# Row-layout loads, a spectrum with the frequency innermost, and two-frequency products in a long-convolution kernel

## The chip, the cores and the metric

The kernel runs on one core of a Trainium2 chip. The metric is the device time of one execution in microseconds. Before the change it was 288.6 us, the median of 3 runs (286.54 to 289.76). Every ratio compares a kernel with the kernel before on the same chip in the same rounds. Experiments of different rounds are compared by these ratios.

## The reference, cut to what matters

```python
# q = k = v: [1, 2048, 512] bf16; shift_k: [512, 4]; ssm_k: [512, 2048]; ssm_D: [512]
k_shift = sum(k_pad[:, t:t+S, :] * shift_k[:, ks-1-t] for t in range(4))   # causal conv of 4 taps
kv   = k_shift * v
kv_f = rfft(pad(kv, 2S));  kf_f = rfft(pad(ssm_k, 2S)).T
y    = irfft(kv_f * kf_f)[:, :S] + kv * ssm_D
h    = x + layernorm(x) * y                     # x = q
out  = h + relu(layernorm(h) @ w1) @ w2
```

The kernel makes each transform in two stages of matrix products. A token is 64 a + b (a and n1 run over 32, b and n2 over 64), and a channel is 128 rg + 64 d + g (four row groups rg, two halves d, 64 g). A "frequency" below is one k1 of the 32 of the first stage.

## The kernel before

"# ..." marks a cut.

```python
# start: tokens in rows of 512 channels, 16 tokens a partition; conv in 8 pieces of 2x512
for c in range(NT // RC):
    acc = pr.tile([P, RC, D], BF16, name="acc")
    # ... 4 multiplies with wbc, 3 adds, all on nc.vector ...
    nc.vector.tensor_tensor(out=vt[:, rr, :], in0=acc[:], in1=vt[:, rr, :], op=ALU.mult)
# ssm_k: 64 TensorE transposes, evicted by ACT into kfl[P, g, d, b]
for q in range(8):
    pst = psum.tile([P, 8, P], BF16, tag="ps", name="pst")
    # ... 8 transposes ...
    nc.scalar.copy(out=kfl[:, :, :, 8*q:8*q+8], in_=pst[:].rearrange("p i (dp g) -> p g dp i", dp=2))
# product k*v: 64 TensorE shuffles into PSUM, then ACT writes the stage's layout
xfl = xflp.tile([P, 64, 2, 64], BF16, name="xfl")        # [g, d, token]
    # ... matmul with ident as lhsT ...
    nc.scalar.copy(out=xfl[:, :, :, n0:n0+4], in_=pcs[a][:].rearrange("p i (dp g) -> p g dp i", dp=2))

kf = slotB.tile([P, DC, 32, 64, 2], F32R, tag="B", name="kf")   # re/im innermost, frequency outside
def store_kf(k1, ps):                                            # D is added here, on DVE
    nc.vector.tensor_tensor(out=kf[:, :, k1, :, 0], in0=ps[:, 0, :]..., in1=dtab_b[:], op=ALU.add)
    nc.scalar.copy(out=kf[:, :, k1, :, 1], in_=ps[:, 1, :]...)

def product(k1, ps):                                             # one frequency at a time
    t12 = prod.tile([P, 2, DC * 64], F32R, name="t12")
    nc.vector.tensor_tensor(out=t12v[:, :, 0:NV, :], in0=u[:, :, 0:NV, :], in1=k_same[:, :, 0:NV, :], op=ALU.mult)
    # ... t34 with re/im swapped; the last quarter of both on nc.gpsimd ...

for t in range(NT):                                              # 16 statistics ahead of the inverse
    nc.vector.bn_stats(out=st1[:, t, :], in_=xh[:, t, :])
    # ...
for g in range(64):                                              # first inverse stage
    nc.tensor.matmul(out=pso, lhsT=kf[:, :, :, g, 0], rhs=dre[:], start=True, stop=False)
    nc.tensor.matmul(out=pso, lhsT=kf[:, :, :, g, 1], rhs=dim[:], start=False, stop=True)
    # ... 3 of 4 evictions on ACT, 1 on DVE ...
```

## Time and profile before

| stage | from (us) | to (us) | limit |
|---|---|---|---|
| set-up, loads, conv | 0 | 42.5 | phases, sines, evictions one behind the other |
| first and second stage of k | 42.5 | 82 | ACT, then TensorE |
| first stage of x | 81.9 | 94.8 | TensorE |
| products with second stage of x | 96.5 | 131.2 | TensorE, DVE near it |
| first inverse stage | 131.9 | 168 | evictions, statistics |
| second inverse stage, MLP | 168 | 287.4 | TensorE |

The time of a stage is read from the first and last matmul of its tile. In profile lines PE is TensorE, PEld its weight loads, DVE VectorE, ACT ScalarE, POOL GpSimd, and L253 is line 253 of the kernel. These are groups of instructions of the kernel before: line, engine, operation, output from inputs, shapes, count, then busy us and mean ns of one, then idle time ahead of them.

```profile
L334 DVE TENSOR_TENSOR t<-ps,kf 128x384 fp32r<-128x384 f32 x32 | 17.6, 550 | 1.9 <-ACT usb L333 1.7
L263 DVE TENSOR_TENSOR vt<-acc,vt 128x1024 bf16<-128x1024 bf16 x8 | 5.4, 685 | 0.0
L283 ACT CAST xfl<-pc 128x512 bf16<-128x512 f32 x16 | 8.4, 1105 | 0.0
L99 PEld LDWEIGHTS <-xfl 32*128 32x128 bf16 x256 | 6.5, 106 | 0.1
```

A product of 384 f32 elements took 550 ns, and the product k*v, 1024 bf16 elements written in order, 685 ns: 0.67 ns an element. The layout of xfl was written by ACT, from PSUM, in runs of 4 tokens.

### The profile page before, as it was taken

How to read it: one execution, taken by the hardware profiler on the slowest of the kernel's cores; microseconds unless marked ns; L12 is line 12 of the kernel's file. 1: busy time of each engine (PE TensorE's matmuls, PEld its weight loads, DVE VectorE, ACT ScalarE, POOL GpSimd, SP SyncE). 2: the span in 40 equal slices, each digit the busy share in tenths (PEclk: the TensorE clock that was granted, in tenths of full speed). 3: DMA queues.
4: the chain of work that ended last, by engine and by line, in shares of the span. 5: the costliest groups of instructions: out<-in, count | busy, mean ns of one | idle time of the engine just before them, and what ended most of it. 6: DMA issues, size and time to landing. Idle time of an engine off the chain costs nothing.

```text
span 287.4 us, 7594 instructions
## 1 busy us (share of the span) xinstructions
PE 225.3 (78%) x3098; PEld 156.9 (55%) x3108; DVE 196.2 (68%) x449; ACT 152.9 (53%) x327; POOL 48.0 (17%) x97
## 2 busy tenths in 40 slices
PE   2027007889986699988999385999999998999994
PEld 0027005529975699977999273544544554444441
DVE  4899999985896599996836936578294258233221
ACT  1039999998885278877966313464352045113000
POOL 9921000000000389983000000000000000000000
PEclk9999555556995599996899757589999999999999
DMA  5699400000000000029156000000000200020122
GB/s 120 150 344 229 98 0 6 5 2 0 2 3 5 2 2 2 2 66 208 22 183 211 0 2 5 2 2 1 5 0 5 57 18 0 18 57 0 38 56 55
DMA packets 7876, 14.25 MB, mean 50 GB/s; under 512 B 2210, under 2 KB 5634, under 8 KB 7714
## 3 DMA queue, kind: packets, MB, share of 16 engines
q1 hardware_dynamic: 4898, 11.31, 15.5%
q10 hardware_dynamic: 2944, 2.46, 3.0%
q8 instruction: 24, 0.39, 0.6%
q14 instruction: 10, 0.08, 0.1%
HBM read 11.67 MB, written 2.10 MB: 48 GB/s over the span
## 4 chain that ended last, share of the span: by engine, by line
PE 60%; ACT 11%; DVE 9%; issue 3%; DMA 2%; ACTq 0%; DVEq 0%; SPq 0%
PE ps2m L465 12%; PE ps1m L454 12%; PE pz L422 7%; ACT a1k L270 5%; PE psi L391 4%; PE psi L392 4%; DVE st L382 3%; PE ps L112 3%; PE ps L114 3%; PE ps L115 3%; PE ps L113 3%; PE pt L444 1%; DMA xh<-in_A_q_dram 1%; ACT xfl L283 1%; DVE a1x L304 1%
## 5 line engine op out<-in xcount | busy, mean ns | idle before, releaser
L454 PE MATMUL ps1m<-hlnT,w 128*128 128x512 bf16 (+1 forms) x169 | 41.6, 387 | 2.1 <-ACT h1T L457 1.0
L465 PE MATMUL ps2m<-w,h1T 128*128 128x512 bf16 (+1 forms) x173 | 38.4, 379 | 0.2
L468 DVE TENSOR_TENSOR o<-ps2m,xh 128x512 bf16<-128x512 f32 x16 | 11.1, 692 | 29.6 <-PE ps2m L465 17.8
L391 PE MATMUL psi<-dre,kf 128*128 128x256 f32 x64 | 26.4, 412 | 5.3 <-DVE bp L396 3.1
L454 PEld LDWEIGHTS <-w 128*128 128x128 bf16 (+1 forms) x176 | 17.0, 102 | 23.2 <-issue 7.8
L457 ACT ACTIVATE h1T<-ps1m 128x512 bf16<-128x512 f32 (+1 forms) x24 | 14.4, 599 | 27.4 <-PE ps1m L454 24.7
L465 PEld LDWEIGHTS <-h1T 128*128 128x128 bf16 (+1 forms) x176 | 17.2, 98 | 20.8
L422 PE MATMUL pz<-bp,ecore 32*32 32x128 f32 x1024 | 25.2, 393 | 3.5 <-ACT zt L428 2.1
L336 POOL TENSOR_TENSOR t<-usb,kf 128x128 fp32r<-128x128 f32 x32 | 15.1, 473 | 73.3 <-ACT usb L333 71.6
L392 PE MATMUL psi<-dim,kf 128*128 128x256 f32 x64 | 25.4, 397 | 0.0
L99 PE MATMUL ps<-f_hi,kfl 32*128 32x64 bf16 x256 | 10.3, 234 | 18.5 <-ACT kfl L230 15.7
L391 PEld LDWEIGHTS psi<-dre,kf 128*128 128x128 f32 x64 | 20.0, 313 | 7.1 <-DVE bp L396 3.4
L394 ACT COPY bp<-psi 128x256 f32<-128x256 f32 x48 | 17.8, 372 | 9.3 <-PE psi L392 7.6
L428 ACT CAST zt<-pz 128x512 bf16<-128x512 f32 x16 | 8.2, 600 | 26.4 <-PE pz L422 26.4
L348 ACT CAST kf<-psy 128x512 fp32r<-128x512 f32 x32 | 20.1, 631 | 3.6 <-POOL t L336 1.4
L422 PEld LDWEIGHTS pz<-bp,ecore 32*32 32x32 f32 x1024 | 15.5, 117 | 10.4 <-issue 4.1
L392 PEld LDWEIGHTS psi<-dim,kf 128*128 128x128 f32 x64 | 20.3, 317 | 0.0
L433 DVE TENSOR_TENSOR gt<-zt,qln 128x512 bf16<-128x512 bf16 x16 | 6.5, 407 | 19.8 <-ACT zt L428 19.8
L334 DVE TENSOR_TENSOR t<-ps,kf 128x384 fp32r<-128x384 f32 x32 | 17.6, 550 | 1.9 <-ACT usb L333 1.7
L459 DVE TENSOR_SCALAR h1T<-ps1m 128x512 bf16<-128x512 f32 x20 | 13.6, 682 | 7.1 <-PE ps1m L454 7.1
L229 PE MATMUL pst<-ident,sk 128*128 128x128 bf16 x64 | 6.7, 299 | 14.0 <-DMA sk<-in_A_ssm_k_dram 14.0
L335 DVE TENSOR_TENSOR t<-ps,kf 128x384 fp32r<-128x384 f32 x32 | 17.5, 548 | 0.0
(133 smaller groups left out, 575.7 us busy)
## 6 DMA issues: line engine op xcount, KB each, us to landing
vt<-in_A_v_dram SPq DMA_DIRECT2D x16, 128.0 KB, 8.4
sk<-in_A_ssm_k_dram SPq DMA_DIRECT2D x1, 2048.0 KB
xh<-in_A_q_dram SPq DMA_DIRECT2D x4, 512.0 KB, 8.4
kh<-in_A_k_dram SPq DMA_DIRECT2D x13, 128.0 KB, 4.5
w<-in_B_w_dram SPq DMA_DIRECT2D x1, 1376.0 KB, 6.4
w<-in_B_w_dram ACTq DMA_DIRECT2D x1, 1280.0 KB, 9.6
out_dram<-o SPq DMA_DIRECT2D x32, 32.0 KB, 1.5
out_dram<-o ACTq DMA_DIRECT2D x32, 32.0 KB, 1.7
```

Of the source, the lines that this page charges most:

```text
L270: _stage1(nc, psum, kfl, f1hi, f1lo, a1k, lambda i, d, s: nc.scalar.copy(out=d, in_=s))
L334: nc.vector.tensor_tensor(out=t12v[:, :, 0:NV, :], in0=u[:, :, 0:NV, :], in1=k_same[:, :, 0:NV, :], op=ALU.mult)
L335: nc.vector.tensor_tensor(out=t34v[:, :, 0:NV, :], in0=u[:, :, 0:NV, :], in1=k_swap(0, NV), op=ALU.mult)
L336: nc.gpsimd.tensor_tensor(out=t12v[:, :, NV:DC, :], in0=usb[:], in1=k_same[:, :, NV:DC, :], op=ALU.mult)
L348: nc.scalar.copy(out=kf[:, :, k1, :, :].rearrange("p r g s -> p s r g"), in_=psy[:].rearrange("p s (r g) -> p s r g", r=DC))
L391: nc.tensor.matmul(out=pso, lhsT=kf[:, :, :, g, 0], rhs=dre[:], start=True, stop=False)
L392: nc.tensor.matmul(out=pso, lhsT=kf[:, :, :, g, 1], rhs=dim[:], start=False, stop=True)
L394: nc.scalar.copy(out=bp[:, g, :, :, :], in_=ps[:])
L422: nc.tensor.matmul(out=pz[32 * a:32 * a + 32, rg, l4, :], lhsT=ecore[rows, rho, n2, :], rhs=rhs, start=(rho == 0), stop=(rho == 1), tile_p ...
L454: nc.tensor.matmul(out=ps1[:fsz, :], lhsT=w1[:, c, fc * P:fc * P + fsz], rhs=hlnT[:, c, sc * SCW:(sc + 1) * SCW], start=(c == 0), stop=(c ...
L457: nc.scalar.activation(out=h1T[:fsz, fc, sc * SCW:(sc + 1) * SCW], in_=ps1[:fsz, :], func=ACT.Relu)
L465: nc.tensor.matmul(out=ps2[:], lhsT=h1T[:ksz, fc, t * P:(t + 1) * P], rhs=w2[:ksz, fc, :], start=(fc == 0), stop=(fc == NFC - 1))
```

## The change

The intent is to take work off the start and off the evictions. k, v and ssm_k are loaded straight into the layout of the first stage (a row group per 32 partitions), so 128 TensorE transposes and shuffles and 24 ACT evictions go away; DVE's product writes xfl itself. D is added by a small matmul in the first stage of k. The spectrum kf is stored as [re/im, g, rg, frequency], so that the first inverse stage loads its weights in order; two frequencies are handled per product. The order of instructions is set by hand. The diff, cut to its core:

```diff
-    kh = pp.tile([P, NT + 3, D], BF16, name="kh")            # 4 KB rows of tokens
+    pieces = [(0, 16), (16, 12), (28, 8), (36, 8), (44, 8), (52, 8), (60, 4)]
+            src = bass.AP(tensor=k_d.tensor, offset=k_d.offset + (n0 - h) * D + P * rg,
+                          ap=[[64 * D, 32], [D, rc + h], [1, P]])                # 256 B pieces
+            nc.sync.dma_start(out=kx[i][rows, 3 - h:rc + 3, :], in_=src)
 # ...
-        nc.scalar.copy(out=kfl[:, :, :, 8 * q:8 * q + 8], in_=pst[:].rearrange("p i (dp g) -> p g dp i", dp=2))
+                src = bass.AP(tensor=A_ssm_k.tensor, ..., ap=[[64, 32], [S, 32], [1, 64]])  # 128 B pieces
+                nc.sync.dma_start(out=kfl[32*rg:32*rg+32, 32*gh:32*gh+32, dp, :], in_=src)
 # ...
+    for pq in (lo, hi):
+        nc.gpsimd.tensor_single_scalar(out=cn[pq, :, pq], in_=cs[pq, :, pq].bitcast(F32), scalar=-1.0, op=ALU.mult)
 # ...
-            nc.scalar.copy(out=xfl[:, :, :, n0:n0 + 4], in_=pcs[a][:].rearrange("p i (dp g) -> p g dp i", dp=2))
+        eng = nc.gpsimd if i == 0 else nc.vector
+        eng.tensor_tensor(out=xfl[:, :, :, n0:n0 + rc].rearrange("p g d n -> p n d g"),
+                          in0=acc[:].rearrange("p n (d g) -> p n d g", d=2),
+                          in1=vx[i][:].rearrange("p n (d g) -> p n d g", d=2), op=ALU.mult)
 # ...
-    kf = slotB.tile([P, DC, 32, 64, 2], F32R, tag="B", name="kf")
+    kf = slotB.tile([P, 2, 64, DC, 32], F32R, tag="B", name="kf")
 # ...
+    def product(kp):
+        u = psum.tile([P, 2, 2, 256], F32, tag="u", name="u")
+        uj = u[:].rearrange("p s k j -> p s j k")
+            t = prod.tile([P, 2, 2, 256], F32R, tag="t%d" % swap, name="t")
+            tj = t[:].rearrange("p s k j -> p s j k")
+                eng.tensor_tensor(out=tj[:, :, j, :], in0=in0, in1=in1, op=ALU.mult)   # pairs of frequencies inside
 # ...
-    for t in range(NT):
-        nc.vector.bn_stats(out=st1[:, t, :], in_=xh[:, t, :])
+    for b in range(16):                       # first inverse stage, four g a block
+        # ... 8 matmuls with lhsT=kf[:, c, 4*b+i, :, :], one eviction of 1024 ...
+        if b >= 8:
+            ln1_stats(b - 8)
```

## The prediction

> **What bounds the kernel now.** I read the page, then the stage table (busy time per stretch), then the groups, waits and DMA packets of single stretches. Columns of the table: stretch, its length, busy us (instructions) of PE, PEld, DVE, ACT, POOL, granted TensorE clock, DMA share, GB/s.
>
> ```profile
> 0.00:16.00 16.00, 1.96 (x4) 0.43 (x4) 10.72 (x17) 1.28 (x1) 13.45 (x22) 1.00 0.61 164
> 16.00:27.00 11.00, 6.74 (x64) 6.60 (x64) 10.96 (x40) 7.54 (x15) 2.82 (x3) 1.00 1.05 276
> 27.00:42.50 15.50, 0.00 (x0) 0.00 (x0) 15.50 (x30) 15.38 (x22) 0.00 (x0) 0.56 0.32 71
> 42.50:59.50 17.00, 13.86 (x535) 9.10 (x536) 16.96 (x30) 15.76 (x34) 0.00 (x0) 0.50 0.02 4
> ...
> 64.00:82.00 18.00, 18.00 (x156) 17.80 (x144) 13.17 (x31) 14.86 (x38) 0.00 (x0) 0.84 0.00 1
> 82.00:96.50 14.50, 8.74 (x513) 6.85 (x512) 10.36 (x17) 8.94 (x18) 0.00 (x0) 0.66 0.02 4
> 96.50:126.50 30.00, 30.00 (x240) 30.00 (x241) 28.49 (x61) 23.55 (x58) 25.99 (x59) 0.93 0.01 2
> ...
> 131.90:154.00 22.10, 22.07 (x97) 21.78 (x98) 10.75 (x26) 17.43 (x44) 1.19 (x2) 0.86 0.57 161
> 154.00:168.00 14.00, 9.00 (x33) 7.42 (x32) 12.55 (x39) 6.10 (x15) 0.00 (x0) 0.78 0.09 28
> ```
>
> The rows are: set-up up to 42.5 us; first stage of k (ACT-bound: 32 evictions at 0.49 us); second stage of k from 64 (PE full); first stage of x; the products (PE full, DVE 28.5 of 30); the first inverse stage, 131.9 to 168. After 168 come second inverse and MLP, 119 us, which the change leaves alone. So no one engine bounds the whole; each stage has its own limit. The waits name three that need not be there:
>
> ```profile
> ACT f_f L67 <- DVE f_aph L60: 15.9, 1, 15.9
> PE ps L99 <- ACT kfl L230: 15.7, 1, 15.7
> DVE bp L396 <- PE psi L392: 12.3, 12, 2.2
> ```
>
> ACT stands idle to 17.9 us because the phase arithmetic is behind convolution work on DVE; then PE waits for the kfl evictions mixed among sines. The chain of waits shows the third loss: from 154.45 to 165.03 it runs through 16 bn_stats (0.66 us apart) with the last evictions of the inverse behind them. And the groups show a slow weight load:
>
> ```profile
> L391 PEld LDWEIGHTS psi<-dre,kf 128*128 128x128 f32 x64 | 20.0, 313 | 7.1 <-DVE bp L396 3.4 <-ACT bp L394 2.7 <-ACT kf L348 1.0
> L112 PEld LDWEIGHTS ps<-a1k,c2c 128*128 128x128 f32 x32 | 7.0, 218 | 0.5 <-issue 0.5
> ```
>
> Strided weights (kf with re/im innermost) take 313 ns, contiguous ones of the same size 218.
>
> [...] Trace: 2752-byte packets of w1 ran at 398 GB/s (110 ns each per engine, 16 engines), 1 KB packets of w2 at 348 (47 ns). A line through both gives 9 ns + 0.037 ns/B, so about 14 ns at 128 B and 18 ns at 256 B. But the only 128-byte packets of this trace, those of dtab_b, ran far below it, with the engines mostly idle (windows 2 to 3 us, then 152 to 154 us):
>
> ```profile
> DMA packets 287, 0.03 MB, mean 35 GB/s; under 512 B 287, under 2 KB 287, under 8 KB 287
> q1 hardware_dynamic: 287, 0.03, 21.4%
> DMA packets 672, 0.70 MB, mean 348 GB/s; under 512 B 0, under 2 KB 671, under 8 KB 671
> q10 hardware_dynamic: 671, 0.69, 108.2%
> ```
>
> That is some 350 packets/us (45 GB/s) once started. All of them read the same 1 KB of HBM, so I cannot tell a limit on packets from a hot spot. This is the main uncertainty. [...] loads to 32 partitions ran at 213 to 233 GB/s with engines full, those to 128 at 348 to 398. Every new k, v and ssm_k load has 32 partitions. [...] Trace: 240 matmuls of 256 columns in 30 us, 125 ns at clock 0.93[...] Trace: 128 elements 0.47 us, started 0.425 apart[...].
>
> **The change part by part.**
> *Start.* Removed: 64 transposes (6.7 us PE), 8 kfl evictions (7.6 us ACT), 64 shuffles of v with 16 evictions (8.4 us ACT), broadcast of the weights over PE, one of 5 DVE operations per pair of phase tables, the third sine table (8 x 0.63 us). Order is by hand: phases and sines first, convolution after. ACT has only 4 sines of 64x2048 (about 2 us each) and is free by some 20 us. Added: packets. ssm_k is read in 16,384 pieces of 128 B, k and v in 19,060 of 256 B (before: mostly 4 KB). By the fitted line: 16,384 x 14/16 + 19,060 x 18/16 ns = 14 + 22 = 36 us[...]. The second half of kfl is behind 24,308 packets: about 28 us. Then half of the first stage of k (8 evictions of 1024 elements at 0.92 = 7.4 us), and 18 us of second stage as now: it ends at about 55 instead of 82. DVE up to there: 4 phase operations of 2048 (4.7), small ones (2)[...]: 45 us, ending about 50 to 58 with waits. So the first stage of x starts at about 58: **-24 us**.
> *First stages.* 32 added matmuls for D lie in other row groups, about 0.3 us per block; ACT (14.7 us against 15.8) stays level with PE (1.7 us per 64 matmuls). First stage of x: the same 512 matmuls, about 14.5 us. **0**.
> *Products.* Per two frequencies PE has 8 matmuls x 0.125 + 4 of 512 columns x 0.24 = 1.96 us, as now 2.0. [...] Fewer instructions, but PE is the limit[...]: 2.1 us x 16 plus 4.5 of filling and tail = 38 us against 35.4. **+2.5**.
> *First inverse stage.* Weights contiguous: 128 matmuls at about 0.14 instead of 0.23 = 18 us instead of 29. Evictions in 16 of 1024. I followed the order of DVE: 16 phase operations (6.6), 8 evictions (1.2 each = 9.6), 14 of the 16 bn_stats still ahead of the last eviction (9.2), waits for ACT 2: 28 us instead of 36. **-8**.
> *Rest.* Same instructions: **0**, 119 us.
> Sum: 288.6 - 24 + 2.5 - 8 = 259.
>
> **The rivals.** *A: a packet limit.* If 350 packets/us holds for all, kfl is complete at 24,308/350 + 2 = 71 us, all 35,444 pieces at 103 us, the first stage of x starts at about 106 instead of 82: 259 + 48 = 307, slower. For it: the dtab_b rows, engines 21% busy. Against: one hot kilobyte, and 1 KB packets reach nearly the same count while limited by their bytes. A milder case (550/us: all in at 66 us) gives some 270. *B: strided access makes products the bound.* kf is then read in pairs 128 B apart and the PSUM tile with its two frequencies 1 KB apart. If DVE ran at half rate, 3.4 us x 16 = 55 us: 259 + 18 = 277. Against: ACT's a1k evictions read PSUM at 256 B steps at 0.49 us per 512 and show nothing; storing kf at 8 B steps costs 443 instead of 372 ns for 256, so a fifth is possible. *C: the load is hidden and DVE is the wall:* scattered 2-byte writes to xfl at half rate add 7 us: 266.
>
> **Range and chances.** I give the mild loading 0.55 (250 to 263), something between 0.2 (263 to 285), rival A nearly in full 0.2 (290 to 307), below 250 0.05. Median about 262, shifted 3 us up from the sum by the rivals. Range 246 to 300.
>
> **What would show it.** Right: 256-byte packets well above 350/us with engines over 60% busy in the first 45 us; first stage of x at 54 to 64 us; psi weight loads near 218 ns and a first inverse stage of 25 to 30 us; product stage 36 to 40 us with PE full. Wrong: DMA share of 0.2 to 0.3 for 70 to 100 us with PE waiting for kfl or DVE for kx (rival A); DVE product operations well over 0.95 us each (rival B); DVE full from 5 us to the first stage of x with xfl writes over 1.5 us for 8 rows (rival C). The prediction fails most if the load order starves k's first stage, since all later stages shift with it one for one.

Terms of its sum: of DVE's 45 us in the start, 31 for the conv and 7 for the scattered product into xfl; in the products, DVE's 1.72 us a pair of frequencies and the chain that took TensorE's 1.96 us to 2.1. A second figure for the loads, 29 us by their bytes: the sum did not use it. With these terms the sum came to 288.6 - 24 + 2.5 - 8 = 259. Rivals B and C double the 1.72 and 7.

From the trace of the kernel before alone I estimate nearly the same. On DVE, phase operations of 512 elements start 0.34 to 0.40 us apart, so the four of 2048 take 5.9 us instead of 4.7; conv instructions of 1024 start 0.60 apart, so 56 of them take 34; products of 384 f32 elements start 0.46 apart, so the 6144 elements of xfl, at that pace, take 7.4: with the small ones 49 us instead of 45. The products of 768 take 0.92 each, 1.84 a pair of frequencies. TensorE's bf16 matmuls of 512 columns in the MLP were busy 0.22 to 0.25 us each (the prediction has 0.24), so 1.96 a pair stands. ACT's copies of 256 elements take 0.37, GpSimd's products of 128 start 0.425 apart: one copy and two products of 256 make 2.07, just over it. ACT's evictions of 512 start 0.49 apart, so the eight of 1024 take 7.8 us instead of 7.4. The steps keep their sizes.

## The result, and the profile after

The changed kernel took 314.48 us (median of 4 runs, 313.4 to 314.86), against 289.17 us for the kernel before in the same rounds: ratio 1.0897, 95% interval 1.0843 to 1.0952, so it is slower by 9%.

The stage table of the changed kernel, with the columns explained in the prediction, from the wait for DVE to the end (the fourth row is the first inverse stage):

```profile
73.00:101.30 28.30, 1.04 (x75) 1.04 (x79) 27.26 (x26) 0.00 (x0) 0.00 (x0) 0.56 0.20 44
100.30:114.70 14.40, 8.68 (x512) 7.35 (x513) 10.29 (x9) 8.27 (x8) 0.80 (x2) 0.50 0.02 5
116.00:163.80 47.80, 35.03 (x188) 26.23 (x187) 45.55 (x32) 22.15 (x32) 23.72 (x33) 0.98 0.00 1
163.80:194.40 30.60, 20.86 (x133) 19.55 (x135) 25.58 (x54) 15.47 (x18) 3.60 (x8) 0.80 0.60 161
194.40:311.30 116.90, 107.65 (x1440) 53.55 (x1440) 59.38 (x155) 34.84 (x74) 0.00 (x0) 0.93 0.08 20
```

In the first row TensorE does next to nothing for 28 us while DVE is full. In the third DVE is full and TensorE is not: the products, which were bound by TensorE, are now bound by DVE. The waits name the same two, among others (engine, line that waits, what it waits for: us in total, times, longest):

```profile
PE ps L274 <- DVE xfl L253: 28.4, 1, 28.4
PE ps L274 <- DMA kfl<-in_A_ssm_k_dram: 20.1, 7, 9.4
ACT kf L309 <- POOL xfl L253: 11.6, 1, 11.6
PE psy L355 <- DVE t L346: 11.1, 16, 0.7
PE pz L453 <- DVE bp L422: 4.8, 1, 4.8
```

The third line is a side effect: ACT's evictions of the second stage of k waited 11.6 us for GpSimd's product into xfl, so that stage ended at 71.8 us.

The groups give the prices (compare with the four lines of the kernel before):

```profile
L346 DVE TENSOR_TENSOR t<-u,kf 128x768 fp32r<-128x768 f32 x32 | 45.6, 1586 | 2.7 <-ACT usb L336 2.7
L253 DVE TENSOR_TENSOR xfl<-acc,vx 128x1024 bf16<-128x1024 bf16 (+2 forms) x6 | 28.3, 4722 | 0.4 <-DMA vx<-in_A_v_dram 0.2
L416 PEld LDWEIGHTS psi<-dre,kf 128*128 128x128 f32 x64 | 15.0, 235 | 6.7 <-ACT bp L424 2.8 <-DVE bp L422 2.2 <-ACT kf L357 1.6
```

The product k*v into xfl takes 4.7 us per 1024 elements where it took 0.69, nearly seven times as long. The product of the spectra takes 1586 ns for 768 elements, where two of the old form (768 elements) took 1100. The weight load of the inverse stage fell from 313 ns to 235 on average.

The rival that had worried me most is gone: the loads ran with the DMA engines full. The packet lines of the stretch from 12 to 20 us:

```profile
DMA packets 8181, 1.17 MB, mean 146 GB/s; under 512 B 8181, under 2 KB 8181, under 8 KB 8181
q1 hardware_dynamic: 8181, 1.17, 108.2%
```

That is 1020 packets/us, three times the 350/us of the dtab_b rows; 16 full engines at 8181 packets in 8 us means 15.6 ns a packet of 143 bytes on average (forecast 14 for 128 B, 18 for 256 B). In the 28 us the DMA engines were busy for 0.20. The DMA excuse is thus ruled out for the 28 us, though not for everything: the second half of kfl landed at about 37 us (forecast 28).

A last thing stands in the timelines (start us, duration us, instruction). DVE:

```profile
19.01 1.22 DVE L250 TENSOR_TENSOR tm<-kx,wj 128x2048 bf16<-128x2048 bf16 x1
21.52 4.69 DVE L250 TENSOR_TENSOR tm<-kx,wj 128x2048 bf16<-128x2048 bf16 x1
27.51 4.54 DVE L250 TENSOR_TENSOR tm<-kx,wj 128x2048 bf16<-128x2048 bf16 x1
40.08 7.02 DVE L253 TENSOR_TENSOR xfl<-acc,vx 128x1536 bf16<-128x1536 bf16 x1
47.54 9.30 DVE L250 TENSOR_TENSOR tm<-kx,wj 128x1024 bf16<-128x1024 bf16 x1
```

GpSimd at the same time:

```profile
19.61 1.80 POOL L215 MEMSET c2n<- 64x2048 f32 x1
21.50 11.20 POOL L220 TENSOR_SCALAR c2n<-c2s 64x2048 fp32r<-64x2048 f32 x2
...
39.34 7.47 POOL L232 TENSOR_SCALAR dim<-dm_f 64x64 fp32r<-64x64 f32 x2
46.90 9.89 POOL L253 TENSOR_TENSOR xfl<-acc,vx 128x2048 bf16<-128x2048 bf16 x1
```

The same DVE instruction takes 1.22 us beside a memset and 4.5 to 4.7 where it meets one of the two GpSimd instructions on c2n, which read SBUF (those that follow, at 26.25 and 32.08 us, took 1.23); one of half the size takes 9.30 us beside GpSimd's scattered product. Whether DVE stands until the GpSimd instruction ends, these lines do not settle: the 9.30 us instruction ended at 56.84 us and GpSimd's at 56.79, but the one that started at 21.52 ended at 26.21, before the GpSimd instruction beside it (21.50 to 26.87); spans on GpSimd are rough. The loss is seen in both directions: GpSimd's two dim instructions took 7.47 us together beside DVE's scattered product (started at 40.08), and 1.93 us in a kernel without it (told below).

### The profile page after: what moved, and what is told of

Same layout as the page of the kernel before. It is cut to its first block, busy times and chain, and to the rows that moved or that the text cites. A ratio compares the mean times of both kernels' runs of the same rounds, so it can differ in the third digit from the quotient of the medians.

```text
span 311.3 us, 6957 instructions
## 1 busy us (share of the span) xinstructions
PE 206.5 (66%) x2944; PEld 136.9 (44%) x2944; DVE 238.0 (76%) x330; ACT 121.6 (39%) x171; POOL 82.7 (27%) x81
## 4 chain that ended last, share of the span: by engine, by line
PE 38%; DVE 36%; SPq 10%; issue 6%; ACT 5%; DMA 3%; POOL 0%; ACTq 0%; DVEq 0%; POOLq 0%
PE ps2m L497 11%; PE ps1m L486 11%; DVE t L346 8%; DVE xfl L253 7%; PE pz L453 6%; DVE tm L250 5%; SPq L119 5%; PE psy L355 3%; SPq L139 3%; DVE acc L251 3%; ACT kf L357 3%; PE psi L416 2%; SPq L142 2%; DVE st L404 2%; DVE bp L422 2%
## 5 line engine op out<-in xcount | busy, mean ns | idle before, releaser
L346 DVE TENSOR_TENSOR t<-u,kf 128x768 fp32r<-128x768 f32 x32 | 45.6, 1586 | 2.7 <-ACT usb L336 2.7
L250 DVE TENSOR_TENSOR tm<-kx,wj 128x1024 bf16<-128x1024 bf16 (+3 forms) x21 | 31.5, 1501 | 0.5
L274 PE MATMUL ps<-f_hi,xfl 32*128 32x64 bf16 x256 | 8.5, 235 | 32.5 <-DVE xfl L253 28.4
L346 POOL TENSOR_TENSOR t<-usb,kf 128x256 fp32r<-128x256 f32 x32 | 23.7, 767 | 23.5 <-PE u L287 16.0
L253 DVE TENSOR_TENSOR xfl<-acc,vx 128x1024 bf16<-128x1024 bf16 (+2 forms) x6 | 28.3, 4722 | 0.4 <-DMA vx<-in_A_v_dram 0.2
L357 ACT CAST kf<-psy 128x1024 fp32r<-128x1024 f32 x16 | 18.9, 1181 | 23.9 <-PE psy L355 23.9
L355 PE MATMUL psy<-t,ipos 128*128 128x512 f32 x48 | 18.1, 431 | 12.6 <-DVE t L346 11.1
L314 ACT CAST a1x<-ps 128x1024 fp32r<-128x1024 f32 x8 | 8.3, 1111 | 33.7 <-PE ps L274 33.7
L292 ACT CAST a1k<-ps 128x1024 fp32r<-128x1024 f32 x16 | 15.4, 1103 | 11.9 <-PE ps L274 11.9
L309 ACT CAST kf<-ps2k 128x1024 fp32r<-128x1024 f32 x15 | 15.0, 1125 | 12.1 <-POOL xfl L253 11.6
```

The source lines that it names most:

```text
L250: nc.vector.tensor_tensor(out=tm[:], in0=src, in1=w, op=ALU.mult)
L253: eng.tensor_tensor(out=xfl[:, :, :, n0:n0 + rc].rearrange("p g d n -> p n d g"), in0=acc[:].rearrange("p n (d g) -> p n d g", d=2), in1=v ...
L274: nc.tensor.matmul(out=pss[rg // 2][:, rg % 2, gi, :], lhsT=src_fl[rows, 8 * gb + gi, :, :].rearrange("p d n -> p (d n)"), rhs=f[rows, :], ...
L292: stage1(kfl, a1k, True, lambda h, o, i: nc.scalar.copy(out=o, in_=i))
L346: eng.tensor_tensor(out=tj[:, :, j, :], in0=in0, in1=in1, op=ALU.mult)
L355: nc.tensor.matmul(out=psy[:, s, :, :].rearrange("p k j -> p (k j)"), lhsT=(ipos if i == 0 else m)[:], rhs=t[:, i, :, :].rearrange("p k j ...
```

## The experiments

Theory S (scatter): writing xfl one 2-byte element at a time, 256 bytes apart, is what makes DVE the wall at the start. Theory L ("lock" in the labels): DVE loses the time to GpSimd. Theory W (write order): the products are slow since t is written one 4-byte element at a time, 1 KB apart. Rivals for the products: reading PSUM at a 1 KB step, or reading kf in pairs 128 bytes apart.

### 1. xfl in the natural order

```diff
-    xfl = xfp.tile([P, 64, 2, 64], BF16, name="xfl")
+    xfl = xfp.tile([P, 2, 64, 64], BF16, name="xfl")       # [d, token, g]
-        eng.tensor_tensor(out=xfl[:, :, :, n0:n0 + rc].rearrange("p g d n -> p n d g"),
+        eng.tensor_tensor(out=xfl[:, :, n0:n0 + rc, :].rearrange("p d n g -> p n d g"),
-                                         lhsT=src_fl[rows, 8 * gb + gi, :, :].rearrange("p d n -> p (d n)"),
+                                         lhsT=xfl[rows, :, :, g].rearrange("p d n -> p (d n)")   # read at a 128-byte step
```

> Changed kernel, but xfl is laid out [d, n, g] so that the convolution product is written in runs of 64 elements, and the first stage of x reads its weights at a 128-byte step. Theory scatter (28.3 us of DVE for 6 products because single 2-byte elements land 256 B apart): each product of 1024 elements falls from 4.7 to about 0.7 us, POOL's from 9.9 to about 4.5; first stage of x starts at about 72 us instead of 101 (then second stage of k is the wall); time about 314 - 29 = 285 us. Rival (the products are slow because of the loads or POOL, not of the writes): products stay over 3 us, time over 305. Side cost: if strided weights are slow, the first stage of x takes over 18 us instead of 14.7.

It took 287.01 us, ratio to before 0.9972 (0.9929 to 1.0015): one layout gives back the whole loss. The instructions that touch xfl (durations are min/median/max in ns, then first and last start):

```profile
L274 PEld LDWEIGHTS <-xfl x512: 161/213/243, 73.0 to 86.5; 32*128 32x128 bf16 x171
L253 DVE TENSOR_TENSOR xfl<-acc,vx x6: 426/692/959, 40.1 to 72.5; 128x1024 bf16<-128x1024 bf16 x4, 128x1536 bf16<-128x1536 bf16 x1, 128x512 bf16<-128x512 bf16 x1
```

The product fell to 692 ns per 1024 elements, and the first stage of x begins at 73.1 us instead of 100.3. The price is on TensorE: weights read at a 128-byte step take 213 ns instead of 127, which costs the stage about a microsecond (first to last matmul 13.4 us against 12.5). Theory S holds.

### 2. GpSimd taken off the conv's side, scatter left

```diff
-        nc.gpsimd.tensor_single_scalar(out=cn[pq, :, pq], in_=cs[pq, :, pq].bitcast(F32), scalar=-1.0, op=ALU.mult)
+        _sin(nc, cn[pq, :, pq], tsn[pq], 8192, MINUS, pq)                # on ACT
-            nc.gpsimd.tensor_single_scalar(out=dst[pq, rho, pq], ...)
+            nc.vector.tensor_single_scalar(out=dst[pq, rho, pq], ...)
-        eng = nc.gpsimd if i == 0 else nc.vector
+        eng = nc.vector
```

> Changed kernel, but POOL does no elementwise work beside the convolution: the negated sine table comes from ACT, the small scalings and the product of piece 0 from DVE; scattered writes stay. Theory lock[...]: the three long DVE operations (4.7, 4.5, 9.3 us) fall to 1.2, 1.2, 0.7 us, 15.4 us less; piece 0 adds about 9.4 us of scattered product on DVE; net about -6: 308 us. Rival (they are long because DMA writes into SBUF or waits for data): the long operations stay, time about 323.

It took 312.37 us, ratio 1.0848 (1.0783 to 1.0914), against 1.0897 for the changed kernel: not told apart. The stalls did go (no multiply or add of the conv over 1.23 us), but two things took their place on DVE, seen in its timeline:

```profile
21.62 0.30 DVE L232 TENSOR_SCALAR dre<-dm_f 64x64 fp32r<-64x64 f32 x2 [4.05 <-POOL dre L228]
31.88 9.26 DVE L253 TENSOR_TENSOR xfl<-acc,vx 128x2048 bf16<-128x2048 bf16 x1
```

DVE now stands for GpSimd's memset of dre, so the conv begins at 23.2 us instead of 17.9 (5.3 us), and does the first piece's scattered product itself (9.3 us). Together 14.6 us, against stalls of 3.5 + 3.3 + 8.6 = 15.4 us removed. The stalls do come from GpSimd, as theory L says, but the 308 us expected were missed by 4, since the wait for the memset was not foreseen. Moving GpSimd's work to DVE gains nothing while the moved product is itself slow; what the stalls alone cost, this run does not tell.

### 3. The same scattered layout, the hops moved to the reads

```diff
-        ...out=xfl[:, :, :, n0:n0 + rc].rearrange("p g d n -> p n d g"), in0=acc[:].rearrange("p n (d g) -> p n d g", d=2),
+        ...out=xfl[:, :, :, n0:n0 + rc].rearrange("p g d n -> p d g n"), in0=acc[:].rearrange("p n (d g) -> p d g n", d=2),   # in1 likewise
```

> Changed kernel, the scattered product iterated with n innermost: writes in runs of 8 to 16 elements, both inputs read single elements 256 B apart. If the cost is in the writes alone: 1024 elements in about 1.2 us, time about 290. If any operand that hops costs as much: still 4 to 5 us (or more, two inputs hop), time 310 to 320.

It took 298.0 us, ratio 1.0352 (one round). The same elements go to the same places; only the order in which they are visited differs, so that writes come in runs and the two reads hop by 256 bytes:

```profile
L253 DVE TENSOR_TENSOR xfl<-acc,vx x6: 1239/2488/3550, 40.1 to 83.8; 128x1024 bf16<-128x1024 bf16 x4, 128x1536 bf16<-128x1536 bf16 x1, 128x512 bf16<-128x512 bf16 x1
```

2488 ns per 1024 elements: two hopping reads cost about half of one hopping write (4712), and still 3.6 times the price of order. Both expectations missed: the cost is neither in the writes alone nor the same for any operand that hops.

### 4. The products' results written in order

```diff
-            t = prod.tile([P, 2, 2, 256], F32R, tag="t%d" % swap, name="t")
-            tj = t[:].rearrange("p s k j -> p s j k")
+            t = prod.tile([P, 2, 256, 2], F32R, tag="t%d" % swap, name="t")   # psy likewise
+            tj = t
```

> Changed kernel, the products t and psy stored with the two frequencies innermost, so that DVE and POOL write t in order; PSUM reads still hop 1 KB between the two frequencies, kf is still read in pairs 128 B apart. Theory write[...]: DVE products start 0.9 to 1.0 us apart, product stage 47.8 -> about 38 us, time about 304. Rival read (hops in PSUM, or pairs of kf): DVE products stay at 1.4 us, time 314.

It took 300.75 us, ratio 1.0449 (1.0394 to 1.0505). The group of the product, and the product stage in the stage table:

```profile
L346 DVE TENSOR_TENSOR t<-u,kf 128x768 fp32r<-128x768 f32 x32 | 29.2, 965 | 7.8 <-ACT usb L336 3.8 <-issue 3.3 <-POOL t L346 0.5
```

```profile
114.50:152.20 37.70, 36.15 (x192) 28.66 (x192) 29.17 (x32) 21.79 (x31) 24.04 (x32) 0.93 0.00 1
```

965 ns instead of 1586, with PSUM still read at a 1 KB step and kf still in pairs 128 bytes apart, so neither read is the cause of the difference. The stage takes 37.7 us (49.0 from its first to its last matmul in the changed kernel), and TensorE is full again. Theory W holds. Taken as a difference per element, a write that hops cost (1586 - 965)/768 = 0.8 ns more than one in order.

### 5. and 6. All three together, and without taking off GpSimd

The first is the sum of edits 1, 2 and 4; the second of 1 and 4.

> Three mended parts together: xfl laid out with the token innermost to the frequency (written in runs of 64 elements), no GpSimd instruction beside the conv, and the product results written in order. Theory (the loss is three costs of DVE access and sharing, one after the other): each saving seen alone should add up until the next wall. The first stage of x waited 9.2 us for DVE in the first mended kernel; without the three stalls of about 3.4 us each and with the first piece's product (1.4 us) back on DVE, that wait goes: PE is then bound by the second stage of k, so the first stage of x starts at 63 to 66 us instead of 73. The product stage takes 36 us instead of 48 as in the kernel with results in order. Sum 287.0 - 8.5 - 11.5 = 267 us, 263 to 271. Rival (the mends hide one another, or there is one more limit in the products, such as PE or GpSimd): 272 to 280 us.

> As the one with all three mends, but with the GpSimd instructions beside the conv left in place, so that the stalls of DVE are priced where the scattered writes no longer hide them. Theory: DVE's chain is again the wall, and the first stage of x starts at about 73 us, 8 to 10 us later than with all three; 275 us, 272 to 279. Rival (the stalls cost nothing once the scatter is gone, since second-stage work fills the time): within 2 us of the kernel with all three.

All three took 270.08 us, ratio 0.9349 (0.9307 to 0.939); without edit 2 it was 275.93 us, ratio 0.9531 (0.9468 to 0.9593). The parts add up: 0.9972 - (1.0897 - 1.0449) = 0.9524 for edits 1 and 4, measured 0.9531. Once the scatter is gone, standing beside GpSimd has a price of its own, 0.0182 of 288.8, or 5.3 us, where experiment 2 had found next to nothing: the same product, moved to DVE, now costs 1.2 us there instead of 9.3. This is the net price of edit 2, whose later start of the conv (23.2 us instead of 17.9) is in it. In the profiles 3.6 us of it lie in the start (first stage of x at 73.3 and 69.7 us, where 8 to 10 us were expected) and 1.7 in the first inverse stage, which the edit does not touch; that part has no explanation. In the second of the two kernels a conv instruction of 0.69 us still takes 4.55 beside GpSimd's product, now one of 4.25 us, and the two dim instructions are short again:

```profile
41.61 4.55 DVE L250 TENSOR_TENSOR tm<-kx,wj 128x1024 bf16<-128x1024 bf16 x1
```

```profile
39.35 1.93 POOL L232 TENSOR_SCALAR dim<-dm_f 64x64 fp32r<-64x64 f32 x2
41.35 4.25 POOL L253 TENSOR_TENSOR xfl<-acc,vx 128x2048 bf16<-128x2048 bf16 x1
```

One step of my expectation failed: with all three mends I put the start of the first stage of x at 63 to 66 us. It began at 69.7, and TensorE still waited for DVE:

```profile
PE ps L274 <- DVE xfl L253: 6.5, 1, 6.5
PE pz L453 <- DVE bp L422: 4.7, 1, 4.7
```

### 7. The statistics behind the last eviction

```diff
-        if b >= 8:
-            ln1_stats(b - 8)
+    for t in range(8):          # after the loop over b
+        ln1_stats(t)
     ln1_rstd(0, 8)
```

> As the one with all three mends, and the eight bn_stats pairs of the first inverse stage put behind the last eviction. In the changed kernel the last eviction on DVE ended at 193.1 us because statistics stood ahead of it in DVE's queue, and PE waited 4.8 us for it. Theory: the second inverse stage starts 2 to 3 us earlier and the statistics then delay its first normalised tile by less than that, so 1 to 3 us less than with all three: 264 to 266. Rival: the sixteen statistics (about 0.75 us each, 12 us) are then all ahead of the first tile's chain on DVE, and the time stays the same or grows by up to 3 us.

It took 269.23 us, ratio 0.9321 (0.9291 to 0.935), within the interval of the kernel with all three mends. The second inverse stage does begin earlier, 23.7 us after the products instead of 29.2, but the rest then takes 123.3 us instead of 116.9, and the wait has a new name:

```profile
PE pz L453 <- ACT zt L460: 7.2, 1, 7.2
PE pz L453 <- DVE bp L422: 1.4, 1, 1.4
```

DVE's work was moved and not removed; the rival was right. This reordering did not win the 4.8 us of that wait.

### 8. ssm_k loaded before k and v

```diff
-    load_kv(0); load_kfl(0); load_kv(1); load_kfl(1)
+    load_kfl(0); load_kfl(1); load_kv(0); load_kv(1)
```

> As the one with all three mends, but both halves of ssm_k are loaded before k and v. With the stalls and the scatter gone the first stage of k waits for its second half, which landed at about 37 us because 128-byte packets of k and v went ahead of it; loaded first, it is complete at about 20 us, at some 1000 packets a us. Theory (loads set the start of PE's chain): the two stages of k end earlier, at about 55 us instead of 64, but the conv's first piece comes about 9 us later, so DVE becomes the wall again: its chain of about 45 us ends at 66 to 70; between -2 and +5 us against the kernel with all three. Rival (PE's chain alone is the wall): 5 to 8 us less.

It took 272.63 us, ratio 0.9448 (0.941 to 0.9487): 2.9 us slower than with the old order (0.0099 of 288.8). The second stage of k ended at 58 us instead of 63, but the last product into xfl came 1.2 us later, and TensorE's wait for DVE became

```profile
PE ps L274 <- DVE xfl L253: 12.3, 1, 12.3
```

So the late ssm_k was not the wall; DVE's chain was.

### 9. The small tables early

```diff
+    # dm_t turns right behind the f1 turns; dm_f, dre, dim ahead of the memsets of cc, cs, cn
-    # (they stood behind the sines of cc, cs, cn)
```

> On top of the kernel with the three mends and the statistics moved: the small tables of the last transform (dm_t, dm_f, dre, dim) are made early, before GpSimd's memsets of the cosine and sine tables, which now follow. In the kernel with all three mends DVE stood 4.0 us for GpSimd's memset of dre, and its four 64-element dm_t operations took 1.74 to 1.87 us each beside GpSimd's memsets, where such an operation took 0.23 to 0.25 us elsewhere; the conv could begin at 23.2 us. Theory (DVE beside GpSimd loses time even in the memsets, and the conv chain still sets the start of the first stage of x at 69.7): the dm_t operations take about 0.25 us each, the conv begins at 13 to 15 us, its later pieces then wait for loads, and the first stage of x starts at about 65 us, where PE's second stage of k (ending at 63) takes over; 3 to 6 us less, 263 to 266. Rival (the loads, all in at about 40 us, with the later pieces after that, set the end of the conv): at most 2 us less.

It took 267.62 us, ratio 0.9281 (0.9232 to 0.933). The dm_t operations are short now, but the loss moved to other one-input operations that stand beside GpSimd's memsets (these ran from 9.21 to 21.41 us in the changed kernel). The two forms on w_r took 1.28 and 1.23 us on w_ts, at 5.58 and 6.89 us, and the dim pair 0.29 in experiment 7:

```profile
4.80 0.25 DVE L54 TENSOR_SCALAR dm_t<-dm_r,n2c_f 128x64 int32<-128x64 int32 x1
8.87 2.90 DVE L54 TENSOR_SCALAR w_r<-w_r,n2c_f 128x2048 int32<-128x2048 int32 x1
11.81 2.79 DVE L56 TENSOR_SCALAR w_r<-w_r 128x2048 int32<-128x2048 int32 x1
14.71 3.53 DVE L208 TENSOR_SCALAR dim<-dm_f 64x64 fp32r<-64x64 f32 x2
22.46 1.23 DVE L246 TENSOR_TENSOR acc<-kx,wj 128x2048 bf16<-128x2048 bf16 x1
```

The conv begins at 22.5 us instead of 23.2, not at 13 to 15. The six memsets of 1.8 us, 10.8 us in all, have to run somewhere, and one-input DVE operations beside them lose the time. By the ratios this is 0.004, or 1.2 us, less than experiment 7 (the intervals overlap), which is the size the rival gave, though the loads are not the cause it was put down to: DVE's set-up beside the memsets is.

### 10. and 11. How long must a run of writes be?

On top of the kernel of experiment 7, xfl is laid out with runs of 2 or 8 channels g innermost (the expectations call them frequencies), and the product is written in those runs. From run to run the step is 512 bytes with pairs (the expectation says 256) and 2048 with eights:

```diff
-    xfl = xfp.tile([P, 2, 64, 64], BF16, name="xfl")
+    xfl = xfp.tile([P, 64 // G, 2, 64, G], BF16, name="xfl")          # G = 2 or 8
+        for d in range(2):
+            eng.tensor_tensor(out=xfl[:, :, d, n0:n0 + rc, :].rearrange("p h n g -> p n h g"), ...)
```

> On top of the kernel with the three mends and the statistics moved: xfl laid out with pairs of frequencies innermost, so that the product is written in runs of two elements (4 bytes) at a 256-byte step, in two instructions of 512 elements a piece of 8 rows. It measures what the scattered write is charged by. Theory A (each hop costs, whatever is written there): half as many hops as single elements, so about 2.3 ns an element, 1.2 us for 512 elements. Theory B (the element is what costs[...]): either 4.6 ns an element (2.4 us for 512), or the full rate, about 0.7 ns an element (0.4 us for 512). Time by A: conv 6 x 1.7 us longer, about 280 us; by the full rate 269.

> The same with runs of eight elements (16 bytes) at a 256-byte step times eight, 512 elements an instruction. Theory A (each hop costs 4.6 ns): 64 hops, 0.3 us and so hidden below the element rate: about 0.4 us for 512 elements, and 270 us in all. Theory B (the element is what costs): 2.4 us for 512 elements, and about 295 us. The weight load of the first stage of x reads at a 16-byte step here, at 4 bytes with pairs, and at 128 bytes with the natural order, where it took 212 ns instead of 127: if the step of the read matters, it lies between.

With pairs it took 270.84 us, ratio 0.9375 (one round); with eights 268.64, ratio 0.9299 (one round). What touches xfl, with pairs:

```profile
L275 PEld LDWEIGHTS <-xfl x512: 97/127/128, 70.3 to 81.9; 32*128 32x128 bf16 x171
L254 DVE TENSOR_TENSOR xfl<-acc,vx x14: 372/636/1050, 31.9 to 69.8; 128x512 bf16<-128x512 bf16 x8, 128x1024 bf16<-128x1024 bf16 x2, 128x768 bf16<-128x768 bf16 x2, 128x256 bf16<-128x256 bf16 x2
```

and with eights:

```profile
L275 PEld LDWEIGHTS <-xfl x512: 135/166/177, 69.2 to 81.4; 32*128 32x128 bf16 x171
L254 DVE TENSOR_TENSOR xfl<-acc,vx x14: 284/426/691, 31.9 to 68.8; 128x512 bf16<-128x512 bf16 x8, 128x1024 bf16<-128x1024 bf16 x2, 128x768 bf16<-128x768 bf16 x2, 128x256 bf16<-128x256 bf16 x2
```

Eights (16 bytes) are written as fast as the natural order (691 ns per 1024 elements, 692 there). Pairs take 1050 ns per 1024, or some 1.0 ns an element, where single elements took 4.6. My theory A had half the price of single elements for pairs (2.3) and theory B all of it or the full rate (0.7); the measurement lies between A and the full rate. So pairs of 4 bytes take away nine tenths of the excess over the ordered write ((4712 - 1050)/(4712 - 692) = 0.91); that the step grew from 256 to 512 bytes as well was not tested apart. Pairs still cost half as much again as the natural order (1050 ns against 692); why, no run shows.

### 12. The version that the runs point to

It is experiment 9 with the runs of eight of experiment 11.

> The version that the runs point to: three mends, statistics behind the last eviction, the small tables early, and xfl with runs of eight frequencies, which were written at the full rate (423 ns for 512 elements) and whose weights loaded in 166 ns instead of 213. Theory (the first stage of x is bound by its weight loads, 512 of them on four row groups that overlap): the stage lasts about 13 us instead of 14.3, so 1 us less than the same kernel with the natural order: 266 to 267 us. Rival (the two-instruction products cost what the loads save): no difference, 267 to 268.

It took 267.3 us (266.8 to 268.75), ratio 0.9288 (0.9232 to 0.9344): 7% faster than the kernel before, and no different from experiment 9. The weight loads are shorter (166 ns), as in experiment 11, and the first stage of x takes 12.3 us instead of 13.4 from its first to its last matmul (512 loads of 166 ns are 85 us, so they do overlap), but the whole gains nothing that these rounds can show.

| kernel | us | ratio to before | first stage of x begins | product stage |
|---|---|---|---|---|
| before | 288.6 | 1 | 81.9 | 35 |
| changed | 314.5 | 1.0897 | 100.3 | 49 |
| 1 natural xfl | 287.0 | 0.9972 | 73.1 | 49 |
| 2 no GpSimd beside the conv | 312.4 | 1.0848 | 99.6 | 49 |
| 4 results in order | 300.8 | 1.0449 | 100.6 | 38 |
| 5 all three | 270.1 | 0.9349 | 69.7 | 37 |
| 12 best | 267.3 | 0.9288 | 68.2 | 37 |

## Why the prediction was wrong

The prediction said 262 us and faster; the measurement was 314.5. From the sum of 259 to the 313.4 us of the profiled run there are 54 us, and they lie almost wholly in two steps.

**Start, -24 forecast, +18.4 measured** (first stage of x at 100.3 instead of 81.9). The step that failed is the DVE sum of 45 us; DVE worked from 2.2 to 100.1 us. Its terms, as they came out:

- The scattered product into xfl for 48 rows, put at 7 us, took 28.3. This is the largest error, 21 us. Rival C had the right mechanism and named the right sign to look for (xfl writes over 1.5 us for 8 rows; they took 4.7), but its size was 7 us more: I allowed for twice the 7 us, and it took four times as long (28.3 us). Experiment 1 shows it: the layout alone brought the start forward by 27 us, in part since GpSimd's own scattered product, and with it the stall of DVE beside it, shrank too.
- Nothing was put down for DVE standing beside GpSimd, though the kernel before showed it: its two DVE operations of 128x128 that started at 7.22 and 7.35 us took 4.47 and 4.41 us and ended with GpSimd's memset of 8.10 to 11.61. In the changed kernel three conv instructions lost 15.4 us, and the set-up of DVE took 15.7 us (2.2 to 17.9) where I had 6.7, with the small operations beside GpSimd's memsets at 1.7 to 1.9 us instead of 0.25. Experiment 6 against 5 prices the GpSimd instructions that read SBUF at 5.3 us net once the scatter is gone; the slow set-up stayed even in the best version, whose first stage of x began at 68.2 us and not at 58.
- The conv was 31 us "with overhead", and is 39.3 without its stalls: instructions of 1024 elements start 0.73 us apart and of 2048 1.26 us (so 0.19 us of each is fixed, by the line through both), seven to a piece; summed over the pieces this is my estimate of 39.3. In the kernel before, where operations of two pieces alternate, such instructions started 0.60 us apart; in the order set by hand each works on the result of the one before it, and only the pair that does not (65.31 and 65.92 us) starts 0.61 apart. No experiment tried to alternate the pieces.
- The loads held: 15.6 ns a packet against 14. The 6.4 MB of the figure for the bytes are 7.0 by the prediction's own piece counts, but the packets were the larger term. kfl was complete at 37 instead of 28 us and the second stage of k ended at 71.8 instead of 55 (63.3 with all three mends), but DVE was later still, and experiment 8 shows that kfl's lateness did not set the end.

**Products, +2.5 forecast, +14.2 measured** (49.0 us from first to last matmul, 34.8 before). The step that failed is "PE is the limit": DVE was, busy for 2.85 us a pair of frequencies (45.6 us over 16). I took DVE's 768-element products at 1.72 us a pair of frequencies (1.84 by the trace of the kernel before), and TensorE as the limit at 2.1. Results in order nearly run so: 965 ns each, 1.83 us a pair, and the stage takes 37.7 us (experiment 4), within half a microsecond of the 38 forecast. What I overlooked is that the results are written to t with the two frequencies 1 KB apart. Rival B had "strided access makes products the bound" and its sign (well over 0.95 us each) came true, but it blamed the reads of kf and PSUM. Those are innocent (965 ns with both as they were, experiment 4); the write is the cause. Its 277 also had 18 us for this where 11.3 were lost.

**First inverse stage, -8 forecast, -6.2 measured** (30.7 against 36.9 us from the last product to the first matmul of the second inverse stage). The mechanism held: weights in order, 235 ns on average instead of 313 (I named 218 as the sign; with the same code 215 in experiment 1 and 191 in experiment 4, so a part of the size is not the layout's). The missing 2 us are not explained by one run; experiment 7 shows only that taking the statistics out of the way gains nothing in the whole.

**Rest, 0 forecast, -2.4 measured** (116.9 against 119.3). No experiment was spent on this.

**Rival A was wrong**: 1020 packets/us against its 350. The dtab_b rows, all reading one kilobyte, were a case of their own; why, no run here shows.

The chances (0.80 for less than 285 us, by its bands) were off for one reason: I gave no weight to the two write patterns together. Both were in the diff, and both had a rival with a sign to look for, but each was sized at a fraction of what it cost.

## What to carry to other kernels

When a shuffle or an eviction is taken away, find who now writes the layout and in what order: an elementwise operation that wrote single 2-byte elements at a 256-byte step ran seven times slower here (4712 ns against 692), while letting TensorE read its weights at a 128-byte step cost 0.09 us a load (213 ns against 127), most of it hidden (13.4 us against 12.5 for the stage), and runs of 16 bytes cost DVE nothing (691 ns). Put the engine's innermost loop along the written operand first, the read operands second: two hopping reads took 2488 ns where one hopping write took 4712. Before giving GpSimd work that reads SBUF beside a full DVE, price it as DVE time, and test such a move again once the larger cost is gone: here the same move won nothing while the moved product took 9.3 us on DVE, and 5.3 us once it took 1.2.

## Prices read from these runs

- DVE's bf16 product of 1024 elements took 692 ns in order, 691 in runs of 8 (16 bytes), 1050 in runs of 2, 4712 for single elements at a 256-byte step, and 2488 when the two reads hopped instead of the write.
- DVE read PSUM at a 1 KB step with 768 f32 elements in 965 ns, so 1.26 ns an element, and a write to SBUF at that step brought it to 1586.
- The GpSimd product of 2048 bf16 elements took 4.26 us in order, 7.58 us with its two reads hopping by 256 bytes and 9.89 us with its write hopping.
- Packets of 143 bytes on average ran at 15.6 ns each with 16 engines full (1020 a us), but the 128-byte packets of dtab_b, which all read the same kilobyte, at only 350 a us with the engines 21 to 31% busy; why stays open.
- In the changed kernel and its variants 32x128 bf16 weights took 127 ns in order and at a 4-byte step, 166 at 16 bytes, 213 at 128 bytes.
